# Decoding float64 weights in PSUM instead of SBUF

## The chip, the core and the metric

The kernel runs on one core of a Trainium2 chip. A core has a matrix engine (TensorE, PE in the profile), a vector engine (VectorE, DVE), an engine for activation functions (ScalarE, ACT), a programmable engine (GpSimd, POOL) and one that only issues transfers (SyncE, SP). Each engine works through its own queue in order and waits on semaphores. [...] The metric is the time of one execution on the device, in microseconds (us).

## What is computed

Local attention over q, k, v (8 batches, 8 heads, 576 positions, 64 per head), then a two-layer block with a gate on its 4608 rows of 512. The weights arrive as float64.

```python
scores = scale * np.matmul(q, k.transpose(0, 1, 3, 2))
mask = (rel >= 0) & (rel < 128)
scores = np.where(mask, scores + bias[None], -1000000000.0)
attn = np.exp(scores - np.max(scores, axis=-1, keepdims=True))
attn = attn / (np.sum(attn, axis=-1, keepdims=True) + 1e-09)
x = np.matmul(attn, v)          # then heads side by side: 4608 x 512
h = x @ w_in                    # 512 x 2048, float64
g = h * (1.0 / (1.0 + np.exp(-1.702 * h)))
out = (g @ w_out).astype(np.float32)   # 2048 x 512, float64
```

## The kernel before

**Second layer block.** The 4608 rows are cut into 18 chunks of 256. A chunk goes through 16 blocks of 128 hidden units. For each block, `up` (L448) makes 12 matmuls into `h_ps`; tanh on ScalarE (L457), the gate on VectorE (L458), a cast on ScalarE (L461) and a subtraction on POOL (L462) give the block's activations as a high and a low part; `down` (L465) makes 6 matmuls into `acc`. Every float32 operand is split in this way into two parts of TensorE's reduced float32 (`fp32r`), and three of the four products are formed.

**Attention.** It runs ahead of the block that consumes it, in units of one or two query blocks of 128. `tick` (L510) advances one step of a software pipeline over the units: scores into `s_ps`, bias, mask and row minimum (`biased`, L321, VectorE), exponent (L332, ScalarE), normalisation (`normal`: L345 on POOL for the first batch's units, L349 on VectorE or L347 on ScalarE for the others), transposes of the weights on TensorE into `t_ps` (`flip`, L364), copies out of `t_ps` (`high`, L375 on ScalarE; `low`, L381 on VectorE), and the product with v into `x_ps` (`mix`). A flip holds one of two `t_ps` buffers from its first transpose to the last of these copies. The first batch's units have no `low`.

**Weights.** Each of 16 blocks has a half of `w_in` and a half of `w_out`: 32 tiles of 128 x 512 float64, 512 KB each, fetched by SP into a resident tile (`fetch`, L201). `decode` (L210) makes two float32 parts of each. It reads a float64 as two 32-bit words. ScalarE scales the top word, read as a float32, by 2^-112 (L218) into `c`, named `wc` in the profile; VectorE shifts the low word right by 29, in place (L219), shifts `c` left by 3 and puts the three low bits in (L220), and puts in the sign (L221). ScalarE rounds the result to the high part (L224), POOL subtracts that from it for the low part (L225). `wc` shares three SBUF buffers under the tag `o` with `xb` (L410).

**Order.** The first block's tiles are decoded during the first batch's attention. The rest are spread over the steps of the block loop (L585), a share of the 32 halves at each step ahead of the ticks, so that each is there when its block is first used. The program's order is a priority: a planner that models the engines puts each engine's queue in order from it, and an instruction whose operands are ready early can be put ahead of others. SP's transfers keep the order in which they are written.

Of the kernel before, what the change touches and what calls it, by code (L numbers as in the profile page):

```python
# [8 lines left out]
F32 = mybir.dt.float32  # L9
F32R = mybir.dt.float32r  # L10
BF16 = mybir.dt.bfloat16
I32 = mybir.dt.int32
I64 = mybir.dt.int64
AF = mybir.ActivationFunctionType
ALU = mybir.AluOpType
PSUM = bass.MemoryType.PSUM
# [4 lines left out]
P = 128  # L21
# [135 lines left out]
def tile_kernel(ctx: ExitStack, tc: tile.TileContext, qT, kT, v, w_in, w_out, out):  # L157
    nc = tc.nc
# [5 lines left out]
    ffn = ctx.enter_context(tc.tile_pool(name="ffn", bufs=2))  # L164
    ps = ctx.enter_context(tc.tile_pool(name="ps", bufs=1, space=PSUM))

    def move(dst, src):

        tc.keep_in_program_order(nc.sync.dma_start(dst, src))
# [4 lines left out]
    bias = [const.tile([P, 2 * P], BF16, name=f"bias{h}") for h in range(H)]  # L174
# [26 lines left out]
    def fetch(src, name):  # L201
        st = const.tile([P, 512], I64, name="r" + name, tag=name)
        move(st, src)
        return st
# [5 lines left out]
    def decode(st, name):  # L210

        words = st.bitcast(I32).rearrange("p (m two) -> p m two", two=2)
        top, low = words[..., 1], words[..., 0]
        c = ffn.tile([P, 512], I32, name="wc", tag="o", bufs=3)

        nc.scalar.activation(c.bitcast(F32), top.bitcast(F32), AF.Copy, scale=2.0 ** -112)  # L218
        nc.vector.tensor_scalar(low, low, 29, None, ALU.logical_shift_right)  # L219
        nc.vector.scalar_tensor_tensor(c, c, 3, low, ALU.logical_shift_left, ALU.bitwise_or)  # L220
        nc.vector.scalar_tensor_tensor(c, top, -0x80000000, c, ALU.bitwise_and, ALU.bitwise_or)  # L221
        w = c.bitcast(F32)
        res = const.tile([P, 2, 512], F32R, name=name, tag=name)
        nc.scalar.copy(res[:, 0], w)  # L224
        nc.gpsimd.tensor_tensor(res[:, 1], w, res[:, 0].bitcast(F32), ALU.subtract)  # L225
        return res


# [99 lines left out]
    def exponents(u):  # L328
        u.sums = att.tile([P, 2], F32, name="sums", bufs=3)
        for e, b in enumerate(u.blocks):  # L330
            live = b.p[:b.rows, b.live:b.end]
            nc.scalar.activation(  # L332
                live, live, AF.Exp, bias=u.mins[:b.rows, e:e + 1], scale=-1.0,
                accum_out=u.sums[:b.rows, e:e + 1],
            )

    def normal(u, on_act):
# [4 lines left out]
        for e, b in enumerate(u.blocks):  # L342
# [3 lines left out]
            elif on_act:  # L346
                nc.scalar.activation(live, live, AF.Copy, scale=u.rec[:rows, e:e + 1])  # L347
            else:
# [92 lines left out]
    class Job:  # L441
# [6 lines left out]
        def up(self, f):  # L448
# [7 lines left out]
            g = ffn.tile([P, T], F32, name="g")  # L456
            nc.scalar.activation(g, h, AF.Tanh, scale=0.851)  # L457
            nc.vector.scalar_tensor_tensor(g, g, 1.0, h, ALU.add, ALU.mult)  # L458
# [97 lines left out]
    while ticks < due[0][0] + 3:  # L556
        tick()
        spin(SPINS)
        fetch_upto(ticks - FETCH_TICK)
        if ticks == DECODE_TICK:  # L560
            w1[0] = decode(w1[0], f"w1_0")
        if ticks == DECODE_TICK + 1:
            w2[0] = decode(w2[0], f"w2_0")
# [21 lines left out]
    for now, (j, f) in enumerate(flat):  # L585

        if halves < 2 * NF:
            owed += max(
                (2 * g + 2 - halves - owed) / max(need[g] - DECODE_AHEAD - now, 1)
                for g in range(halves // 2, NF))  # L590
            while owed >= 1 and halves < 2 * NF:
                owed -= 1
                g, ws = halves // 2, (w1, w2)[halves % 2]
                fetch_upto(g + 1 + FETCH_AHEAD)
                ws[g] = decode(ws[g], f"w{1 + halves % 2}_{g}")
                halves += 1
# [64 lines left out]
```

## Time and profile before

| | |
|---|---|
| median of 3 runs | 1099.26 us (1097.17 to 1099.34) |
| span of the profiled execution, first to last instruction | 1094.0 us |
| the median over that span | 5.3 us |
| mean granted TensorE clock | 0.990 of full speed |
| decoding, first start to last start | 21.98 to 165.09 us |
| HBM read, written | 70.39 MB, 9.44 MB |

The profiled execution's own time on the clock of the runs isn't listed; its span stands for it, and the 5.3 us are what lies around the span if that execution was a median one.

A group row of the profile reads: line, engine, operation, what it writes and reads, shapes, how often; then the busy time and the mean duration of one in ns; then the engine's idle time just before these instructions and what ended it. In a row of single durations stand minimum, median and maximum in ns, then the first and last start in us. A waiting row reads: who waited for whom, us in total, how often, the longest. Rows of busy times in windows give, for each engine, the busy time and the number of instructions, then the granted clock, the share of the DMA engines and their rate.

### The profile page before, as it was taken

To read this page: it belongs to the slowest core of one execution; us is meant where nothing else is said; L and a number is where in the kernel's file an instruction comes from. 1 tells how busy PE (TensorE), PEld (TensorE's weight loads), DVE (VectorE), ACT (ScalarE), POOL (GpSimd) and SP (SyncE) were. 2 spreads that over 40 slices of the span, in tenths; PEclk is the share of its full clock that TensorE was granted. 3 is DMA by queue.
4 is the path that set the end of the run, shared out by engine and by line. 5 is a ranking of instruction groups with operands and counts; after the bars stand their busy time and mean duration, and the time that the engine had idled before them with its cause. 6 is when DMAs were issued, how large, how long until landed. Compare 5 with 4: busy or idle time off the path is not lost.

```text
span 1094.0 us, 21796 instructions
## 1 busy us (share of the span) xinstructions
PE 1059.8 (97%) x7021; PEld 944.6 (86%) x7021; DVE 745.2 (68%) x2331; ACT 592.2 (54%) x1765; POOL 658.9 (60%) x931
## 2 busy tenths in 40 slices
PE   8888889999999999999999999999999999999998
PEld 5565668999998999999999998999999999998997
DVE  4999798778898687754575768676877677423131
ACT  4665565566675665543555556655565556322222
POOL 4998877567677666644565666665666666323232
PEclk9999889999999999999999999999999999999999
DMA  5965213232242222201222222221222212000000
GB/s 142 332 171 160 69 46 86 72 82 74 84 105 86 65 84 65 84 23 48 54 67 53 84 55 84 65 84 51 73 76 65 76 46 78 1 20 20 1 20 19
DMA packets 97265, 81.24 MB, mean 74 GB/s; under 512 B 50048, under 2 KB 88448, under 8 KB 97152
## 3 DMA queue, kind: packets, MB, share of 16 engines
q1 hardware_dynamic: 91968, 70.42, 23.4%
q10 hardware_dynamic: 5184, 9.44, 2.3%
q8 instruction: 55, 0.90, 0.4%
q14 instruction: 58, 0.48, 0.1%
HBM read 70.39 MB, written 9.44 MB: 73 GB/s over the span
## 4 chain that ended last, share of the span: by engine, by line
PE 82%; DVE 3%; issue 1%; POOL 0%; ACT 0%; DVEq 0%; POOLq 0%
PE h_ps L452 34%; PE acc L471 34%; PE x_ps L398 5%; PE s_ps L309 5%; PE t_ps L364 4%; DVE pb L349 0%; DVE xh L436 0%; DVE pb L321 0%; DVE K L294 0%; DVE rec L340 0%; DVE xf L429 0%; DVE wc L221 0%; DVE g L458 0%; DVE pl L381 0%; DVE o L487 0%
## 5 line engine op out<-in xcount | busy, mean ns | idle before, releaser
L452 PE MATMUL h_ps<-xh,w 128*128 128x256 f32 x2304 | 370.5, 285 | 8.8 <-DVE g L458 4.2
L462 POOL TENSOR_TENSOR gl<-g,gh 128x256 fp32r<-128x256 f32 x288 | 218.6, 759 | 262.2 <-ACT gh L461 198.2
L452 PEld LDWEIGHTS h_ps<-xh,w 128*128 128x128 f32 x2304 | 329.5, 189 | 41.2 <-DVE g L458 6.6
L471 PE MATMUL acc<-w,gh 128*128 128x512 f32 x1152 | 326.8, 401 | 1.1 <-DVE xf L479 1.1
L458 DVE SCALAR_TENSOR_TENSOR g<-g,h_ps 128x256 f32<-128x256 f32 x288 | 119.4, 415 | 181.3 <-ACT g L457 179.6
L457 ACT ACTIVATE g<-h_ps 128x256 f32<-128x256 f32 x288 | 109.8, 382 | 209.7 <-PE h_ps L452 192.4
L471 PEld LDWEIGHTS acc<-w,gh 128*128 128x128 f32 x1152 | 197.6, 189 | 28.7 <-issue 1.3
L452 PE MATMUL h_ps<-xl,w 128*128 128x256 f32 x1152 | 195.9, 281 | 0.0
L461 ACT CAST gh<-g 128x256 fp32r<-128x256 f32 x288 | 116.7, 405 | 145.9 <-DVE g L458 136.4
L471 PE MATMUL acc<-w,gl 128*128 128x512 f32 x576 | 189.0, 403 | 0.0
L332 ACT ACTIVATE pb<-pb,mins 128x256 f32<-128x256 f32 (+3 forms) x292 | 141.2, 484 | 64.9 <-DVE mins L321 61.7
L296 POOL TENSOR_TENSOR K<-rk,K 128x384 fp32r<-128x384 f32 (+1 forms) x140 | 127.3, 909 | 80.7 <-ACT Q L276 24.9
L452 PEld LDWEIGHTS h_ps<-xl,w 128*128 128x128 f32 x1152 | 164.2, 189 | 5.8 <-DVE xl L438 0.3
L321 DVE CUSTOM_DVE_ANT_0 pb<-s_ps,bias 128x256 f32<-128x256 f32 (+5 forms) x320 | 114.2, 376 | 14.7 <-PE s_ps L309 6.5
L349 DVE TENSOR_SCALAR pb<-pb,rec 128x256 f32<-128x256 f32 (+2 forms) x252 | 110.1, 473 | 3.5
L295 POOL TENSOR_TENSOR Q<-rq,Q 64x256 fp32r<-64x256 f32 (+1 forms) x140 | 98.0, 700 | 21.6 <-ACT Q L276 4.4
L364 PE MATMUL t_ps<-ident,pb 128*128 128x128 f32 (+1 forms) x548 | 100.8, 275 | 8.2 <-DVE pb L349 6.6
L471 PEld LDWEIGHTS acc<-w,gl 128*128 128x128 f32 x576 | 93.0, 190 | 8.0 <-issue 0.5
L340 DVE TENSOR_SCALAR rec<-sums 128x2 f32<-128x2 f32 (+2 forms) x164 | 55.1, 336 | 59.6 <-ACT pb L332 58.4
L309 PE MATMUL s_ps<-K,Q 128*128 128x256 f32 (+1 forms) x504 | 91.9, 290 | 2.6 <-POOL gl L462 1.4
L381 DVE TENSOR_TENSOR pl<-t_ps,ph 128x512 fp32r<-128x512 f32 (+2 forms) x140 | 84.0, 602 | 5.2 <-ACT ph L375 4.8
L294 DVE CAST K<-rk 128x384 fp32r<-128x384 f32 (+1 forms) x140 | 59.0, 422 | 41.0 <-PE s_ps L309 31.6
(56 smaller groups left out, 1305.7 us busy)
## 6 DMA issues: line engine op xcount, KB each, us to landing
rk<-kT SPq DMA_DIRECT2D x84, 192.0 KB, 2.7
rq<-qT SPq DMA_DIRECT2D x112, 128.0 KB, 2.6
out<-o ACTq DMA_DIRECT2D x36, 256.0 KB, 2.1
rw<-w_in SPq DMA_DIRECT2D x16, 512.0 KB, 5.9
rw<-w_out SPq DMA_DIRECT2D x16, 512.0 KB, 7.0
rk<-kT SPq DMA_DIRECT2D x56, 128.0 KB, 2.3
rv<-v SPq DMA_DIRECT2D x100, 64.0 KB, 2.0
rq<-qT SPq DMA_DIRECT2D x44, 64.0 KB, 2.4
```

The lines of the kernel that those rows point to most:

```text
L296: nc.gpsimd.tensor_tensor(K2, rk, K1.bitcast(F32), ALU.subtract)
L309: nc.tensor.matmul(u.s[:b.rows, e, b.first:b.end], u.Q[:, b.q0 - u.q0:b.q0 - u.q0 + b.rows], k[:, ko:ko + b.end - b.first], start=(z == 0) ...
L321: nc.vector.tensor_tensor_reduce(b.p[ra:rb, cs:b.end], u.s[ra:rb, e, cs:b.end], bias[head][ra:rb, cs:b.end], -SCALE, BIG, ALU.add, ALU.min ...
L332: nc.scalar.activation(live, live, AF.Exp, bias=u.mins[:b.rows, e:e + 1], scale=-1.0, accum_out=u.sums[:b.rows, e:e + 1],)
L349: nc.vector.tensor_scalar(live, live, u.rec[:rows, e:e + 1], None, ALU.mult)
L364: nc.tensor.transpose(u.t[:c.n, w:w + b.rows], b.p[:b.rows, col:col + c.n], ident[:b.rows, :b.rows])
L452: nc.tensor.matmul(h, w1[f][:, z, k * P:(k + 1) * P], x[:, k], start=(n == 0), stop=(n == len(ops) - 1))
L457: nc.scalar.activation(g, h, AF.Tanh, scale=0.851)
L458: nc.vector.scalar_tensor_tensor(g, g, 1.0, h, ALU.add, ALU.mult)
L461: nc.scalar.copy(gh, g)
L462: nc.gpsimd.tensor_tensor(gl, g, gh.bitcast(F32), ALU.subtract)
L471: nc.tensor.matmul(acc, g[:, t * P:(t + 1) * P], w2[f][:, z], start=(f == self.f0 and n == 0), stop=(f == self.f1 - 1 and n == 2))
```

## The change

The decoding's intermediate values move from the SBUF tile `c` to a PSUM tile `bits` that takes its buffer from the two of `t_ps`. The low bits come from a ScalarE activation that reads the upper 16 bits of the low word as an unsigned integer, scales it by 2^-13 and writes an integer in place, instead of VectorE's shift. The two bit steps stay on VectorE, with one operand in PSUM and the other in SBUF. The last subtraction goes from POOL to VectorE, with one operand in PSUM.

```diff
+U16 = mybir.dt.uint16
...
         top, low = words[..., 1], words[..., 0]
-        c = ffn.tile([P, 512], I32, name="wc", tag="o", bufs=3)
-        nc.scalar.activation(c.bitcast(F32), top.bitcast(F32), AF.Copy, scale=2.0 ** -112)
-        nc.vector.tensor_scalar(low, low, 29, None, ALU.logical_shift_right)
-        nc.vector.scalar_tensor_tensor(c, c, 3, low, ALU.logical_shift_left, ALU.bitwise_or)
-        nc.vector.scalar_tensor_tensor(c, top, -0x80000000, c, ALU.bitwise_and, ALU.bitwise_or)
-        w = c.bitcast(F32)
+        part = st.bitcast(U16).rearrange("p (m four) -> p m four", four=4)[..., 1]
+        bits = ps.tile([P, 4 * P], F32, name="w_ps", tag="t_ps", bufs=2).bitcast(I32)
+        nc.scalar.activation(bits.bitcast(F32), top.bitcast(F32), AF.Copy, scale=2.0 ** -112)
+        nc.scalar.activation(low, part, AF.Copy, bias=2.0 ** -14 - 0.5, scale=2.0 ** -13)
+        nc.vector.scalar_tensor_tensor(bits, bits, 3, low, ALU.logical_shift_left, ALU.bitwise_or)
+        nc.vector.scalar_tensor_tensor(bits, top, -0x80000000, bits, ALU.bitwise_and, ALU.bitwise_or)
+        w = bits.bitcast(F32)
         res = const.tile([P, 2, 512], F32R, name=name, tag=name)
         nc.scalar.copy(res[:, 0], w)
-        nc.gpsimd.tensor_tensor(res[:, 1], w, res[:, 0].bitcast(F32), ALU.subtract)
+        nc.vector.tensor_tensor(res[:, 1], w, res[:, 0].bitcast(F32), ALU.subtract)
         return res
```

## The prediction

> **What bounds the kernel now.** I read the page's first two parts, then a table by stretches, then the groups inside the stretch that differs, then the waits there. The page:
>
> ```profile
> span 1094.0 us, 21796 instructions
> PE 1059.8 (97%) x7021; PEld 944.6 (86%) x7021; DVE 745.2 (68%) x2331; ACT 592.2 (54%) x1765; POOL 658.9 (60%) x931
> PE   8888889999999999999999999999999999999998
> DVE  4999798778898687754575768676877677423131
> POOL 4998877567677666644565666665666666323232
> ```
>
> Over the whole span TensorE is the bound. Each slice is 27 us; only the first six show PE below 9, and there VectorE and POOL stand at 7 to 9. That is where decoding runs: its first instruction starts at 21.98 us, its last at 165.09. The busy times of that stretch, and of a later one as long:
>
> ```profile
> core 0: us, PE busy (x) PEld busy (x) DVE busy (x) ACT busy (x) POOL busy (x), PEclk, DMA share, GB/s
> 22.00:165.00 143.00, 117.86 (x646) 87.58 (x645) 131.67 (x319) 87.69 (x237) 121.78 (x114) 0.93 0.54 160
> 313.00:456.00 143.00, 141.70 (x979) 129.77 (x979) 112.39 (x387) 88.65 (x276) 95.84 (x151) 1.00 0.29 78
> ```
>
> The counts say more than the busy times: PE finishes 646 matmuls where later it finishes 979 in the same time. By count, its work up to 165 would fit into 646/979 of 143, some 94 us, so about 49 us are lost there (an estimate, since the mix differs). VectorE is busy 131.7 of 143, 92%; POOL 85%; ScalarE only 61%. Who waits for whom in that stretch:
>
> ```profile
> ACT gh L461 <- DVE g L458: 11.6, 8, 3.4
> ACT w L224 <- DVE wc L221: 11.0, 11, 3.2
> ACT pb L332 <- DVE mins L321: 10.8, 13, 1.8
> PE t_ps L364 <- DVE pb L349: 6.0, 5, 2.0
> PE h_ps L452 <- DVE g L458: 3.7, 5, 1.3
> ```
>
> The longest waits end on VectorE. It sets the pace of 22 to 165 us; after that PE does, and a microsecond won before 165 is one won at the end. What VectorE and POOL spend there:
>
> ```profile
> L220 DVE SCALAR_TENSOR_TENSOR wc<-wc,rw 128x512 int32<-128x512 int32 x32 | 29.0, 907 | 1.0 <-ACT wc L218 0.6
> L221 DVE SCALAR_TENSOR_TENSOR wc<-rw,wc 128x512 int32<-128x512 int32 x32 | 25.7, 803 | 0.1
> L219 DVE TENSOR_SCALAR rw<-rw 128x512 int32<-128x512 int32 x32 | 22.7, 709 | 1.6 <-DMA rw<-w_out 1.1 <-DMA rw<-w_in 0.5
> L349 DVE TENSOR_SCALAR pb<-pb,rec 128x256 f32<-128x256 f32 (+2 forms) x12 | 7.5, 669 | 0.2
> L294 DVE CAST K<-rk 128x384 fp32r<-128x384 f32 (+1 forms) x9 | 5.4, 604 | 6.0 <-POOL w L225 3.3 <-POOL K L296 1.2 <-issue 0.9
> L436 DVE CAST xh<-xf 128x256 fp32r<-128x256 f32 x4 | 3.9, 1013 | 0.2 <-PE h_ps L452 0.2
> L225 POOL TENSOR_TENSOR w<-wc,w 128x512 fp32r<-128x512 f32 x31 | 44.3, 1439 | 5.5 <-ACT w L224 4.4 <-DVE pb L349 1.1
> ```
>
> Decoding takes 29.0 + 25.7 + 22.7 = 77.4 of VectorE's 131.7, and 44.3 of POOL's 121.8.
>
> **The change part by part.** Durations of single instructions, minimum/median/maximum:
>
> ```profile
> L219 DVE TENSOR_SCALAR rw<-rw x32: 399/426/2573, 22.0 to 103.7; 128x512 int32<-128x512 int32 x32
> L220 DVE SCALAR_TENSOR_TENSOR wc<-wc,rw x32: 662/775/1680, 23.1 to 161.8; 128x512 int32<-128x512 int32 x32
> L221 DVE SCALAR_TENSOR_TENSOR wc<-rw,wc x32: 671/684/1415, 25.6 to 163.5; 128x512 int32<-128x512 int32 x32
> L381 DVE TENSOR_TENSOR pl<-t_ps,ph x140: 397/676/694, 131.2 to 940.9; 128x512 fp32r<-128x512 f32 x80, 128x384 fp32r<-128x384 f32 x36, 128x256 fp32r<-128x256 f32 x24
> L218 ACT ACTIVATE wc<-rw x32: 647/670/712, 22.0 to 161.1; 128x512 f32<-128x512 f32 x32
> L224 ACT CAST w<-wc x32: 604/621/636, 26.3 to 164.4; 128x512 fp32r<-128x512 f32 x32
> ```
>
> *Removed on VectorE:* L219, 22.7 us. *Bit steps, L220 and L221:* their operands in SBUF stretch them from 0.66 to as much as 1.68 us while POOL works. L381 has the operand mix that they get, one from PSUM and one from SBUF, and in 140 executions beside POOL it never passed 0.694. I take 0.69 for each: 64 x 0.69 = 44.2 instead of 54.7. A VectorE write into PSUM is in no row; the ends are 0.662 (L220's minimum) and 0.907 (its mean, if the stretch stayed), that is 42.4 to 58.0. I go by L381, the nearest row. *Added subtraction:* the very operation of L381 at its largest shape, 32 x 0.68 = 21.8. VectorE's decoding is then 44.2 + 21.8 = 66.0 instead of 77.4, 11.4 less; with 58.0 for the steps it would be 79.8, 2.4 more.
>
> [...]
>
> *POOL:* 44.3 of 121.8 us go, 36%. Other VectorE work is stretched too: L349 669 ns against its later 457, L294 604 against 422, L436 1013 against 294:
>
> ```profile
> L349 DVE TENSOR_SCALAR pb<-pb,rec 128x256 f32<-128x256 f32 (+2 forms) x231 | 97.3, 457 | 3.2
> L294 DVE CAST K<-rk 128x384 fp32r<-128x384 f32 (+1 forms) x140 | 59.0, 422 | 41.0 <-PE s_ps L309 31.6
> L436 DVE CAST xh<-xf x68: 278/294/1829, 89.2 to 1042.2; 128x256 fp32r<-128x256 f32 x68
> ```
>
> That is 12 x 0.21 + 9 x 0.18 + 4 x 0.72 = 7.0 us; I credit POOL's 36%, 2.5 us. VectorE then needs 131.7 - 11.4 - 2.5 = 117.8 us.
>
> *ScalarE:* the low bits add 32 instructions of L218's kind and shape, 32 x 0.67 = 21.4 us, to 87.7: 109.1. That is hidden: 76% of 143, 85% of 128. A 16-bit read and an integer write are in no row; between 0.604 and 0.712 (L224's least, L218's most) the sum moves by 2 us, and even doubled (130.5) it would only then equal VectorE's present load. If ScalarE's slack were gone, the whole 21.4 would show.
>
> *The buffer:* decoding leaves `wc` (three buffers, shared with `xb`) for `t_ps`, whose two buffers belong to the flips. This adds waits: the first activation waits for a free `t_ps`, with the exponents (L332) and tanh (L457) queued behind it on ScalarE; a flip's transposes (L364) wait for a decoding's subtraction, with the matmuls L452 and L471 behind them on PE. How long a buffer is held now, from rows of the first and last decoding (first activation to the end of L224) and of a short and a long flip:
>
> ```profile
> 21.98 0.69 ACT L218 ACTIVATE wc<-rw 128x512 f32<-128x512 f32 x1
> 26.34 0.62 ACT L224 CAST w<-wc 128x512 fp32r<-128x512 f32 x1
> ...
> 161.06 0.68 ACT L218 ACTIVATE wc<-rw 128x512 f32<-128x512 f32 x1 [1.31 <-DVE xf L429]
> 164.39 0.62 ACT L224 CAST w<-wc 128x512 fp32r<-128x512 f32 x1 [0.46 <-DVE wc L221]
> ```
>
> ```profile
> 30.56 0.27 PE L364 MATMUL t_ps<-ident,pb 128*128 128x128 f32 x1
> 32.21 0.48 ACT L375 COPY pw<-t_ps 128x384 f32<-128x384 f32 x1 [1.61 <-PE t_ps L364]
> 159.29 0.44 PE L364 MATMUL t_ps<-ident,pb 128*128 128x128 f32 x2
> 163.07 0.54 DVE L381 TENSOR_TENSOR pl<-t_ps,ph 128x384 fp32r<-128x384 f32 x1
> ```
>
> So 4.98 and 3.95 us; over all 32 the mean is 5.85. The flips hold 2.1 and 4.3 us; the 24 of this stretch sum to some 64. The least a decoding can hold is its own work, 0.67 + 0.69 + 0.69 + 0.62 + 0.68 = 3.35. Halfway between that and the present 5.85 + 0.68 + 1.17 = 7.7 (1.17 is the mean wait between L220's end and L221's start, as a price for one more turn in VectorE's queue) is 5.5: then the buffers are needed (32 x 5.5 + 64)/2 = 120 us, not quite the bound, but tight. No DMA is moved, and the fetches on SP keep their order.
>
> *Sum:* VectorE is idle 143 - 131.7 = 11.3 us now. With ScalarE fuller and the buffers tight I let that grow by half, to 16.9: the stretch lasts 117.8 + 16.9 = 134.7, **8.3 us less**. The span would go from 1094.0 to 1085.7. The runs' median, 1099.26, is 5.3 over that span (the runs reach 1097.17 to 1099.34); I subtract from the median: **1091.0**.
>
> **The rivals.** *Larger gain:* POOL is a second bound in places; from 54.92 to 72 us it has no idle time, and flips wait for its normalisation (L345) behind L225:
>
> ```profile
> 54.92 3.15 POOL L225 TENSOR_TENSOR w<-wc,w 128x512 fp32r<-128x512 f32 x2
> 58.05 2.96 POOL L345 TENSOR_SCALAR pb<-pb,rec 128x256 f32<-128x256 f32 x2
> ```
>
> With both relieved VectorE could run at 96%: 117.8/0.96 = 122.7, 20 us less, 1079. Against it: ScalarE would be 89% busy, and the two would wait for each other.
>
> *Slower, the buffers:* one mechanism, `t_ps` in decoding's hands. It decides where (32 x hold + 64)/2 passes 143: at a mean hold of 6.9 us. At the 7.7 of today's rows the stretch becomes (246 + 64)/2 = 155 us, 12 more: 1111. For it: today's holds, and that a ready decoding takes any free buffer ahead of a flip that is not yet ready. Against it: part of the present hold is VectorE's stretch and crowding, which shrink.
>
> *No change:* VectorE is relieved, but the flips' waits put back what it wins, hold about 6.9: 1099 within 2 us.
>
> **How the numbers follow.** Forecast 0.47; larger gain 0.15; no change 0.13; buffers 0.25. The forecast's own range lets VectorE's idle time stay at 11.3 (129.1, so 1085) or double (140.4, so 1097). The 8-in-10 range reaches from just below the larger gain to most of the slower case, 1077 to 1108; it also holds the dearer bit steps (13.8 us back, 1105). A measurement here tells about 0.2% (2.2 us) from no change; by that, faster 0.62, same 0.13, slower 0.25.
>
> **What would show it.** Right: bit steps and subtraction at 0.66 to 0.70 with no long maxima, low bits near 0.67 on ScalarE, the last decoding's end near 157, PE full from then on, POOL near 77 us. Wrong: waits of L364 or of the first activation that end on decoding's subtraction, adding up to more than 10 us; bit steps above 0.8; or ScalarE over 90% with VectorE waiting for it. A loss after 200 us would contradict the whole argument, since nothing of decoding runs there.

## The result and the profile after

| | changed kernel | kernel before, same chip |
|---|---|---|
| median of 4 runs | 1088.26 us (1082.55 to 1091.07) | 1098.51 us (1097.17 to 1099.34) |
| ratio | 0.9904, 95% interval 0.9875 to 0.9933 | |
| span of the profiled execution | 1086.3 us (that execution took 1088.07) | 1094.0 us |

The change makes the kernel about 10 us, 1.0%, faster. (The kernel before has a fourth run here, so its median is 1098.51, not 1099.26.) The span lies 1.8 us under the time of its own execution. So most of the 5.3 us between the earlier median and span means that the profiled execution of the kernel before was a faster one than the median. The page of the changed kernel, in its first two parts:

```profile
span 1086.3 us, 21750 instructions
PE 1063.2 (98%) x7021; PEld 945.7 (87%) x7021; DVE 722.8 (67%) x2331; ACT 606.7 (56%) x1797; POOL 596.2 (55%) x899
PE   8988999999999999999999999999999999999998
DVE  4488789888988787744576768776868677413131
POOL 4334556766776676554565656666666565323232
PEclk9599999999999999999999999999999999999999
```

Both kernels do the same work outside decoding, so the totals compare directly: VectorE 745.2 to 722.8, POOL 658.9 to 596.2, ScalarE 592.2 to 606.7. The second slice shows something that the kernel before has not: TensorE's clock is granted at about half (0.53 from 22 to 50 us, where the kernel before has 0.94). The decoding's groups on VectorE, over the whole execution:

```profile
L219 DVE SCALAR_TENSOR_TENSOR w_ps<-w_ps,rw 128x512 int32<-128x512 int32 x32 | 22.0, 692 | 7.2 <-ACT w_ps L217 4.5 <-ACT rw L218 2.1
L220 DVE SCALAR_TENSOR_TENSOR w_ps<-rw,w_ps 128x512 int32<-128x512 int32 x32 | 21.8, 684 | 0.1
L224 DVE TENSOR_TENSOR w<-w_ps,w 128x512 fp32r<-128x512 f32 x32 | 21.7, 682 | 3.0 <-ACT w L223 2.7
```

That is 65.5 us where decoding took 77.4. The busy times by stretches, of the kernel before and then of the changed one (columns as in the prediction):

```profile
22.00:50.00 28.00, 22.20 (x119) 14.91 (x118) 26.44 (x69) 18.20 (x46) 22.49 (x18) 0.94 1.04 316
50.00:80.00 30.00, 25.87 (x131) 18.98 (x129) 28.89 (x64) 17.96 (x45) 29.28 (x24) 0.94 0.71 219
80.00:110.00 30.00, 25.81 (x153) 18.19 (x152) 28.84 (x74) 17.88 (x52) 24.69 (x23) 1.00 0.49 147
110.00:140.00 30.00, 24.13 (x136) 19.34 (x135) 24.16 (x63) 17.82 (x53) 25.80 (x31) 0.89 0.28 76
140.00:170.00 30.00, 24.85 (x151) 20.97 (x152) 28.18 (x70) 18.80 (x53) 24.28 (x27) 0.89 0.15 39
```

```profile
22.00:50.00 28.00, 24.83 (x74) 13.60 (x73) 11.79 (x43) 15.16 (x39) 8.70 (x11) 0.53 0.76 235
50.00:80.00 30.00, 26.71 (x148) 19.94 (x147) 25.94 (x63) 26.70 (x62) 9.85 (x13) 0.98 0.75 242
80.00:110.00 30.00, 26.21 (x161) 19.22 (x160) 24.31 (x77) 24.25 (x65) 14.48 (x19) 1.00 0.57 177
110.00:140.00 30.00, 30.00 (x188) 24.71 (x188) 23.70 (x63) 19.16 (x58) 15.04 (x22) 1.00 0.26 71
140.00:170.00 30.00, 27.68 (x179) 24.66 (x179) 27.88 (x85) 21.86 (x62) 16.77 (x27) 0.94 0.25 64
```

Read the number of PE's matmuls. From 50 to 170 us the changed kernel finishes 676 where the kernel before finishes 571 (the sums of four rows each), 105 ahead; at some 6.8 a microsecond (979 in 143 us of the prediction's later stretch) that is 15 us won. From 22 to 50 us it finishes 74 against 119: 6.6 us lost before anything is won. There VectorE is busy 11.8 of 28 us, less than half of before. ScalarE's rows in that hole (raw starts, durations, the idle time before):

```profile
28.63 0.68 ACT L218 ACTIVATE rw<-rw 128x512 int32<-128x512 uint16 x1
...
30.49 0.48 ACT L374 COPY pw<-t_ps 128x384 f32<-128x384 f32 x1
30.87 0.67 ACT L218 ACTIVATE rw<-rw 128x512 int32<-128x512 uint16 x1
34.74 0.40 ACT L331 ACTIVATE pb<-pb,mins 128x128 f32<-128x128 f32 x1 [3.20 <-DVE mins L320]
...
35.14 0.65 ACT L218 ACTIVATE rw<-rw 128x512 int32<-128x512 uint16 x1
...
39.41 0.48 ACT L374 COPY pw<-t_ps 128x384 f32<-128x384 f32 x1 [3.13 <-PE t_ps L363]
...
45.16 0.48 ACT L374 COPY pw<-t_ps 128x384 f32<-128x384 f32 x1 [3.73 <-PE t_ps L363]
...
47.09 0.61 ACT L217 ACTIVATE w_ps<-rw 128x512 f32<-128x512 f32 x1
```

L218 makes the low bits and needs no `t_ps`; it goes on, so the weights have landed. L217 fills the `t_ps` buffer, one of the PSUM tiles that take the result of every matmul in this kernel; its second execution starts at 25.06 us and its third at 47.09, though ScalarE idles for 3 us and more three times in between. What runs on `t_ps` meanwhile are the flips and their copies (L374). Decoding halts for 22 us. The flips' transposes on TensorE in that time:

```profile
28.65 1.81 PE L363 MATMUL t_ps<-ident,pb 128*128 128x128 f32 x6 [0.70 <-DVE w L224]
...
36.27 0.42 PE L363 MATMUL t_ps<-ident,pb 128*128 128x128 f32 x1
...
38.63 0.69 PE L363 MATMUL t_ps<-ident,pb 128*128 128x128 f32 x2
...
44.17 0.90 PE L363 MATMUL t_ps<-ident,pb 128*128 128x128 f32 x3
```

The buffers are not full. The copy at 30.49 ends the last of the first flips at 30.97 us, and the next transpose starts at 36.27; the next gap runs from 39.89 (the end of the copy at 39.41) to 44.17. In these 9.6 us no instruction works on `t_ps` at all, and still the third decoding does not start. It waits for its turn, not for space.

### The profile page after: what moved, and what is told of

It reads as the page before. It is cut to its first block, busy times and chain, and to the rows that moved or that the text cites. A ratio compares the mean times of both kernels' runs of the same rounds, so it can differ in the third digit from the quotient of the medians.

```text
span 1086.3 us, 21750 instructions
## 1 busy us (share of the span) xinstructions
PE 1063.2 (98%) x7021; PEld 945.7 (87%) x7021; DVE 722.8 (67%) x2331; ACT 606.7 (56%) x1797; POOL 596.2 (55%) x899
## 4 chain that ended last, share of the span: by engine, by line
PE 83%; DVE 2%; ACT 0%; issue 0%; DVEq 0%; POOL 0%; POOLq 0%
PE h_ps L451 34%; PE acc L470 34%; PE x_ps L397 5%; PE s_ps L308 5%; PE t_ps L363 5%; DVE pb L348 0%; DVE xl L437 0%; DVE pb L320 0%; DVE rec L339 0%; DVE pl L380 0%; DVE xf L428 0%; DVE K L293 0%; DVE xh L435 0%; ACT pb L331 0%; DVE g L457 0%
## 5 line engine op out<-in xcount | busy, mean ns | idle before, releaser
L461 POOL TENSOR_TENSOR gl<-g,gh 128x256 fp32r<-128x256 f32 x288 | 215.2, 748 | 278.1 <-ACT gh L460 217.4
L363 PE MATMUL t_ps<-ident,pb 128*128 128x128 f32 (+1 forms) x548 | 101.7, 277 | 3.7 <-DVE w L224 2.9
L339 DVE TENSOR_SCALAR rec<-sums 128x2 f32<-128x2 f32 (+2 forms) x164 | 49.4, 301 | 64.8 <-ACT pb L331 63.7
```

The source lines that it names most:

```text
L363: nc.tensor.transpose(u.t[:c.n, w:w + b.rows], b.p[:b.rows, col:col + c.n], ident[:b.rows, :b.rows])
L461: nc.gpsimd.tensor_tensor(gl, g, gh.bitcast(F32), ALU.subtract)
```

## The experiments

The theories. **Load:** the gain is VectorE's load, as predicted. **POOL:** the gain is the work taken off POOL. **Shared buffer:** sharing `t_ps` costs part of what is won, either throughout or in the **early halt**. **Cold start:** the halved clock is itself the cost. All ratios are to the kernel before on the same chip, with 95% intervals.

**1. The change in parts.** Subtraction alone, low bits alone, both without PSUM, and PSUM with VectorE's shift:

```diff
# e1, kernel before
-        nc.gpsimd.tensor_tensor(res[:, 1], w, res[:, 0].bitcast(F32), ALU.subtract)
+        nc.vector.tensor_tensor(res[:, 1], w, res[:, 0].bitcast(F32), ALU.subtract)
# e2, kernel before
-        nc.vector.tensor_scalar(low, low, 29, None, ALU.logical_shift_right)
+        nc.scalar.activation(low, part, AF.Copy, bias=2.0 ** -14 - 0.5, scale=2.0 ** -13)
# e3, changed kernel
-        bits = ps.tile([P, 4 * P], F32, name="w_ps", tag="t_ps", bufs=2).bitcast(I32)
+        bits = ffn.tile([P, 512], I32, name="wc", tag="o", bufs=3)
# e4, changed kernel
-        nc.scalar.activation(low, part, AF.Copy, bias=2.0 ** -14 - 0.5, scale=2.0 ** -13)
+        nc.vector.tensor_scalar(low, low, 29, None, ALU.logical_shift_right)
```

> Kernel before, with only the last subtraction moved from POOL to VectorE, everything in SBUF. If VectorE's load sets the pace (theory of load): 32 x 0.68 to 0.80 = 22 to 26 us come to VectorE's 131.7, less some 2.5 to 10 us of stretch that POOL's 44 us caused: slower, 1105 to 1115. If POOL's load was the bound (theory of POOL): faster, near 1090.

> Kernel before, with only the low bits moved from VectorE to ScalarE; wc stays in SBUF and the subtraction on POOL. Theory of load: 22.7 us leave VectorE, 10 to 20 us faster, 1080 to 1088, as much as the whole change or more. Theory of POOL: POOL still has its 122 us, under 5 us faster.

> The changed kernel with its intermediate in the old SBUF buffers (three, shared with xb) instead of t_ps: low bits on ScalarE, subtraction on VectorE. It takes the PSUM operand away and gives the flips their two buffers back. If the port mix matters (bit steps stretched by POOL): bit steps at 0.75 to 0.85 us on the mean, VectorE 5 to 8 us more than in the changed kernel, 1092 to 1098. If the shared t_ps holds the changed kernel back by more than that: faster, under 1085.

> The changed kernel with the low bits back on VectorE as a shift of the SBUF word; bit steps in PSUM and subtraction on VectorE. Theory of load: 32 x 0.42 to 0.70 = 13 to 22 us come back to VectorE: 1098 to 1108. If the changed kernel has VectorE to spare (77% busy in its decoding stretch): within 4 us of it, 1084 to 1092.

| run | median us | ratio, interval |
|---|---|---|
| e1, subtraction on VectorE | 1089.90 | 0.9920 (0.9896 to 0.9943) |
| e2, low bits on ScalarE | 1090.00 | 0.9919 (0.9893 to 0.9945) |
| e3, both, all in SBUF | 1076.16 | 0.9791 (0.9771 to 0.9811) |
| e4, PSUM, shift on VectorE | 1091.53 | 0.9934 (0.9914 to 0.9954) |

e1 refutes the plain theory of load: an engine that was 92% busy is given 32 more instructions and the kernel gains 9 us. The decoding stretch of e1, and two of its rows:

```profile
22.00:165.00 143.00, 127.33 (x703) 97.97 (x702) 127.47 (x348) 87.47 (x239) 87.08 (x82) 0.90 0.53 159
L220 DVE SCALAR_TENSOR_TENSOR wc<-wc,rw x32: 662/678/1207, 22.1 to 156.9; 128x512 int32<-128x512 int32 x32
L225 DVE TENSOR_TENSOR w<-wc,w x32: 662/678/1224, 27.3 to 161.9; 128x512 fp32r<-128x512 f32 x32
```

VectorE runs 348 instructions instead of 319 in this stretch and is busy 127.5 us instead of 131.7. The bit step's median falls from 775 to 678 ns. So part of VectorE's busy time was stretch of its instructions while POOL worked, and that part goes with POOL's. Whether POOL's own queue or this stretch was worth more of the 9 us, e1 doesn't separate. Low bits alone (e2) give 9 us too: under the 10 to 20 of the theory of load, over the 5 of the theory of POOL. So neither engine alone held the kernel back. The two edits together (e3) give 22.7, more than their sum.

The surprise is e3: without PSUM the kernel is 12 us faster than the changed one, although its bit steps stretch again (up to 1.24 and 1.31 us). The last expectation of e3 holds: the shared `t_ps` costs more than the operand mix brings. (What it calls the port mix is, as measured, where the operands lie; no run shows ports.) e4 lies within 4 us of the changed kernel, as its second expectation has it, and the two intervals overlap: the changed kernel has room on VectorE for the shift.

**2. Hold time, flips, clock.** In e5 `t_ps` holds only the scaled word; the first bit step writes SBUF:

```diff
# e5, changed kernel
-        nc.vector.scalar_tensor_tensor(bits, bits, 3, low, ALU.logical_shift_left, ALU.bitwise_or)
-        nc.vector.scalar_tensor_tensor(bits, top, -0x80000000, bits, ALU.bitwise_and, ALU.bitwise_or)
-        w = bits.bitcast(F32)
+        c = ffn.tile([P, 512], I32, name="wc", tag="o", bufs=3)
+        nc.vector.scalar_tensor_tensor(c, bits, 3, low, ALU.logical_shift_left, ALU.bitwise_or)
+        nc.vector.scalar_tensor_tensor(c, top, -0x80000000, c, ALU.bitwise_and, ALU.bitwise_or)
+        w = c.bitcast(F32)
# e6, e3's kernel
-        u.t = ps.tile([P, 4 * P], F32, name="t_ps", bufs=2)
+        u.t = ps.tile([P, 4 * P], F32, name="t_ps", bufs=1)
# e7, changed kernel; e8, e3's kernel
-SPINS = 3
+SPINS = 6
```

> The changed kernel, but only the scaled top word goes into the t_ps buffer; the first bit step reads it there and writes the old SBUF buffers, and the rest works in SBUF. A decoding then holds t_ps from the first activation to the end of the first bit step, near 2 us instead of 5.4. Theory of the shared buffer (the flips, and with them the attention, wait for decodings): most of the 12 us between the changed kernel and the all-in-SBUF one comes back, 1076 to 1081. Theory of the cold start (the halved clock from 24 to 51 us does it): nothing to do with the hold, 1084 to 1090.

> The all-in-SBUF kernel (1076) with one t_ps buffer for the flips instead of two. In the changed kernel decodings hold 174 us of buffer time in 146 us, 1.2 of the two buffers, up to 168 us; here the flips lack one buffer through the whole kernel. Theory of the shared buffer: 1083 to 1095, at least half of the 12 us, and the exponents of the first batches late by 5 us or more. If flips hardly need the second buffer: within 3 us of 1076.

> The changed kernel with 6 instead of 3 idle matmuls after each tick of the first batch, which keep TensorE busier up to some 50 us. Theory of the cold start: the halved stretch from 24 to 51 us goes or shrinks to under 7 us, 1080 to 1084. Theory of the shared buffer: the clock may change, the time stays within 3 us of 1088.

> The all-in-SBUF kernel (1076, half clock for 13.7 us from 26 us) with 6 instead of 3 idle matmuls after each tick. Theory of the cold start: 1070 to 1074. If a few microseconds at half clock are covered by other work: 1075 to 1079.

| run | median us | ratio, interval |
|---|---|---|
| e5, short hold of t_ps | 1076.30 | 0.9829 (0.9784 to 0.9874) |
| e6, all in SBUF, one flip buffer | 1085.97 | 0.9895 (0.9868 to 0.9923) |
| e7, changed, 6 idle matmuls | 1094.06 | 0.9963 (0.9942 to 0.9984) |
| e8, all in SBUF, 6 idle matmuls | 1072.40 | 0.9772 (0.9752 to 0.9792) |

e5 brings the 12 us back with a mean hold of 2.8 us instead of 5.4 (one of its four runs took 1084.68). Its decoding halts too, but only to 38.11 us, and catches up: the tenth high part is begun at 59.70 us, in the changed kernel at 70.43. The theory of the shared buffer stands. The cold start as a cause of its own falls with e7. In the decoding stretch, the changed kernel and then e7, and e7's second and third first activation:

```profile
22.00:165.00 143.00, 130.43 (x707) 97.12 (x707) 108.62 (x311) 103.94 (x273) 61.51 (x84) 0.90 0.53 161
22.00:165.00 143.00, 125.15 (x725) 96.64 (x725) 108.35 (x309) 104.34 (x272) 61.24 (x84) 0.96 0.54 162
26.33 0.63 ACT L217 ACTIVATE w_ps<-rw 128x512 f32<-128x512 f32 x1
...
44.35 0.62 ACT L217 ACTIVATE w_ps<-rw 128x512 f32<-128x512 f32 x1
```

The clock goes from 0.90 to 0.96, VectorE stays as idle as it was, decoding still halts for 18 us, and the kernel is 6 us slower, not faster. So the halved clock is not what makes the halt; why e7 is slower, outside both of its expectations, stays open. Where decoding does not halt, the same edit seems to help a little: e8 lies 25.3 us under the kernel before on its chip and e3 22.7 us, with intervals that overlap.

e6 has the expected time for a reason that wasn't expected. With a single buffer for the flips and none of it lent, the decoding stretch runs better than with two: 804 matmuls from 22 to 165 us against e3's 766. It loses later, from 300 to 340 us. There, e3 and then e6:

```profile
300.00:340.00 40.00, 38.70 (x263) 34.72 (x262) 34.57 (x116) 25.15 (x80) 27.86 (x42) 1.00 0.31 87
300.00:340.00 40.00, 33.14 (x204) 28.79 (x203) 35.13 (x118) 24.41 (x76) 26.63 (x44) 0.87 0.32 91
```

So during decoding the flips don't need the second buffer. It isn't the flips that suffer from sharing; it is decoding.

**3. Early or throughout.** The first 10 decodings in one memory, the other 22 in the other, and the control of the idle matmuls:

```diff
# e9, changed kernel (e10: < in place of >=)
+        if len(decoded) >= 10:
+            bits = ps.tile([P, 4 * P], F32, name="w_ps", tag="t_ps", bufs=2).bitcast(I32)
+        else:
+            bits = ffn.tile([P, 512], I32, name="wc", tag="o", bufs=3)
+        decoded.append(name)
# e11, kernel before; e12, e9's kernel
-SPINS = 3
+SPINS = 6
```

> The changed kernel with the first 10 of the 32 decodings in the old SBUF buffers and the other 22 in t_ps. In the changed kernel no decoding starts between 25 and 47 us, while the flips of the first batch take the t_ps buffers in turn; in the all-in-SBUF kernel five start there, and after the fourth block of the second layer both run at one pace (97.5 and 98.0 us for the next 20 blocks). Theory of the early halt: most of the 12 us comes back, 1076 to 1081. Theory of sharing throughout: only 10 of 32 decodings are helped, 1084 to 1088.

> The mirror: the first 10 decodings in t_ps, the other 22 in the old SBUF buffers. Theory of the early halt: 1084 to 1090, like the changed kernel, though 22 decodings share nothing. Theory of sharing throughout: two thirds of the 12 us come back, 1078 to 1082.

> The kernel before with 6 instead of 3 idle matmuls after each tick of the first batch: what the same edit does where decoding keeps VectorE full. If it helps only where VectorE and POOL leave TensorE something to do: within 3 us of 1098. If the clock alone is worth what it gave the all-in-SBUF kernel: 1093 to 1095.

> The kernel with the first 10 decodings in SBUF and the others in t_ps (1077), with 6 instead of 3 idle matmuls after each tick of the first batch. The same edit took the all-in-SBUF kernel from 1076 to 1072 and cost the changed kernel, whose decoding halts early, 6. If what counts is that decoding runs on from 25 us: 1072 to 1076. If later flips and decodings in t_ps eat the gain of a warm clock: 1077 to 1082.

| run | median us | ratio, interval |
|---|---|---|
| e9, first 10 in SBUF | 1077.28 | 0.9802 (0.9780 to 0.9824) |
| e10, first 10 in t_ps | 1095.04 | 0.9981 (0.9961 to 1.0001) |
| e11, before, 6 idle matmuls | 1098.53 | 1.0005 (0.9990 to 1.0020) |
| e12, e9 with 6 idle matmuls | 1073.31 | 0.9761 (0.9741 to 0.9781) |

Ten decodings moved away from `t_ps` bring back 11 of the 12 us; twenty-two bring back none. First activations of e9, then of e10, from 25 us on (only these; the rows between them are left out):

```profile
25.45 0.67 ACT L223 ACTIVATE wc<-rw 128x512 f32<-128x512 f32 x1 [1.11 <-DMA rw<-w_out]
28.21 0.68 ACT L223 ACTIVATE wc<-rw 128x512 f32<-128x512 f32 x1
30.38 0.68 ACT L223 ACTIVATE wc<-rw 128x512 f32<-128x512 f32 x1
34.45 0.69 ACT L223 ACTIVATE wc<-rw 128x512 f32<-128x512 f32 x1
37.73 0.67 ACT L223 ACTIVATE wc<-rw 128x512 f32<-128x512 f32 x1
```

```profile
25.45 0.62 ACT L223 ACTIVATE w_ps<-rw 128x512 f32<-128x512 f32 x1
47.28 0.60 ACT L223 ACTIVATE w_ps<-rw 128x512 f32<-128x512 f32 x1
...
121.92 0.68 ACT L223 ACTIVATE wc<-rw 128x512 f32<-128x512 f32 x1
161.67 1.23 ACT L223 ACTIVATE wc<-rw 128x512 f32<-128x512 f32 x2
```

In e9 decoding runs on; in e10 it halts until 47 us, as in the changed kernel. The early halt is shown. e10 is even slower than the changed kernel by 7 us, outside both of its expectations; its clock in the stretch is 0.81 and decoding pauses once more from 122 to 162 us, so its size mixes several things. e11 shows that idle matmuls alone give the kernel before nothing. e12 and e8, 1073.31 and 1072.40, both beat the kernel before and the changed one; between them the intervals overlap, and those of e12 and e9 just touch.

## Why the prediction was right, point by point

- **Forecast 1091.0, measured 1088.26.** Direction, size and likeliest case came out, but two terms of the sum were too small by similar amounts, and they pull in opposite directions. The forecast took 13.9 us of relief less 5.6 of added idle time; by the runs the relief without the shared buffer is 22.7 us (e3) and sharing costs 12. That the total came so close is partly luck.
- **The bit steps** at 0.69 us each, by the row of L381: measured 0.692 and 0.684 on the mean, with no long maxima. The subtraction at 0.68: measured 0.682. At 128x512 and by medians the subtraction took 681 ns with a PSUM source here and 678 in e1 with both in SBUF.
- **VectorE's relief was sized too small.** The prediction took 11.4 us from decoding (measured 77.4 - 65.5 = 11.9) and credited 2.5 for the stretch of other work, 13.9 in all. The total fell by 22.4. Most of the rest lies in other VectorE work that POOL had stretched: the row of L340 falls from 55.1 to 49.4 us (336 to 301 ns), that of L436 from 31.5 to 25.9 (522 to 439 ns). In e1, where only the subtraction moves off POOL, they fall too, to 49.7 and 28.0; in e2, where POOL keeps it, they don't (54.5 and 32.3). POOL likewise fell by 62.7 where its 44 to 46 us of subtraction went: in the stretch it stands at 61.5 us, not near 77.
- **"It sets the pace" was half the truth.** e1 shows that VectorE's 92% contained stretch beside POOL (the bit step L220 at a median of 775 ns, in e1 678), and that taking work off POOL pays even when VectorE gets it. The prediction had POOL as a rival for a larger gain, not as part of the gain.
- **VectorE's idle time was sized too small as well, and the stretch did not shorten.** The prediction put the stretch at 117.8 busy + 16.9 idle = 134.7 us. From the first decoding's start to the last one's end the changed kernel takes 145.9 us (22.55 to 168.44), of which VectorE is busy 112.1 and idle 33.8; the kernel before takes 144.4 (21.98 to 166.39). So "a microsecond won before 165" was not won by ending the stretch sooner. It was won inside it: TensorE does 726 matmuls there instead of 657, and 69 more are some 10 us of later work.
- **The buffer's price was reckoned by the wrong quantity.** The mean hold was put at 5.5 us and measured 5.43; by that sum the two buffers suffice. But the sum is a mean over the stretch, while the cost sits between 25 and 47 us and is set by whose turn the buffers are. The flips of the first batch come earlier in the program than the third decoding (two are decoded in that loop, the others in the block loop behind it); it gets a buffer only behind them, ready or not. The prediction had it the other way round, that a ready decoding takes any free buffer ahead of a flip that is not yet ready. Its sign for trouble was of that kind too: the waits of L363 and of the first activation for a decoding's subtraction sum to 5.1 + 2.2 = 7.3 us, under its 10, while sharing cost 12. That the order of turns comes from the program's order is read from the kernel and the rows above; putting the third decoding ahead of these flips was not tried, and whether the buffers' order or that of ScalarE's queue holds it back isn't separated.
- **ScalarE** took the low bits at a median of 674 ns (0.67 predicted) with time to spare: busy 103.9 of 143 us.
- **What would show it:** the last decoding was to end near 157 us; it ends at 168.4, for the halt. From 140 to 170 us TensorE is busy 27.7 of 30, full from then on.

## What to carry to other kernels

When a step is moved into the buffers of another, don't stop at the mean hold: look at which of the two asks first in the program, and whether the one that could run ahead loses its own buffers at the moment when the engines that it uses have time. VectorE's busy time beside POOL contained stretch here (L220: minimum 662 ns, mean 907), so compare the same operation's minimum with its mean before taking 92% for a full engine. Of three edits that go together, time each alone: here two were worth 23 us and the third cost 12.

## What the runs showed of the hardware

- A VectorE bit step with both operands in SBUF stretched to 1.68 us beside POOL (the five that ran while POOL was idle took 0.70 at most); with one operand and the result in PSUM, in 64 executions of the changed kernel, it never passed 0.703. POOL also has less to do there, but with the same edits and both operands in SBUF (e3) it still reached 1.31:

```profile
L219 DVE SCALAR_TENSOR_TENSOR w_ps<-w_ps,rw x32: 671/699/703, 23.8 to 163.1; 128x512 int32<-128x512 int32 x32
L220 DVE SCALAR_TENSOR_TENSOR w_ps<-rw,w_ps x32: 675/684/697, 24.7 to 164.4; 128x512 int32<-128x512 int32 x32
```

- ScalarE was a little faster on PSUM for 128x512, by medians: writing it 632 ns against 670 for SBUF (L217 now, L218 before), reading it 583 against 621 (L223 now, L224 before).
- The activation that reads 16-bit integers at a stride of 8 bytes and writes 32-bit ones in place took what the float one took: 674 ns (L218 now) against 670 (L218 before), by medians.
